# Scores ten groups ahead, the first chunk staged in an idle buffer, and row tiles placed under the weight loads

## The chip, the cores and the metric

The kernel runs on one core of a Trainium2 chip. The metric is the device time of one execution in microseconds. The engines are TensorE (PE, with its weight loads shown apart as PEld), VectorE (DVE), ScalarE (ACT), GpSimd (POOL) and the queue of SyncE (SP), which issues most of the DMAs.

## What is computed

An attention with two mixings over the heads, and two feed-forward parts behind it, all in float32:

```python
# q, k, v: (4, 12, 448, 64); w_pre, w_post: (12, 12)
scores = scale * np.matmul(q, k.transpose(0, 1, 3, 2))
scores = np.einsum('bhij,hg->bgij', scores, w_pre)       # mix of the heads before the softmax
attn   = softmax(scores, axis=-1)
attn   = np.einsum('bhij,hg->bgij', attn, w_post)        # mix of the heads behind it
x      = np.matmul(attn, v)                              # -> (1792, 768)
h      = ((x @ w1) * (x @ w2)) @ w3 @ w_out              # 768 -> 1024 -> 1024 -> 768
out    = leaky_relu(h @ w_in, 0.01) @ w_out2             # 768 -> 2048 -> 768
```

The weights come as float64 and are turned to float32 on the chip.

## The kernel before, in words

**Attention.** Each of the 4 batches is cut into chunks of 120, 120, 120 and 88 query rows, a chunk into blocks of 10 rows, and two blocks make a group: 6, 6, 6 and 5 groups a batch, 92 in all, numbered through. A chunk's scores are made per pair of heads in `qk` (L178): two matmuls into PSUM (L187), eviction into an `s` tile (L183, five buffers; L195 on ACT, L193 on DVE in the start-up), then one DMA per head (`move`, L203 to L215; two for the last head) that lays the 120 rows of that head out so that (row, head) stands on the partitions of a row tile `sr` (L126, three of them in turn). The list `reads` collects these DMAs. `premix` (L236) multiplies a group's row tile by the pre-mixing matrix (L247); it reads a row tile that all 13 moves of the chunk write, so a chunk's first `premix` waits for the last of them. Then `tops` (L257, row maxima on DVE), `softmax` (L264, exponentials on ACT), `weigh` (L269 to L282: sum, reciprocal L274, four scalings L280 and L278, three of them on POOL), `postmix` (L300 on PE, L307 transposes on DVE into an `ap` tile, L291, two buffers) and `av` (L324, the product with v, copied out by L333 and stored to `scr`).

**The loop.** One step takes two groups, k and k+1, for k = 0, 2, ... 90, and a last step k = 92 does only the post-mixing. In the order of PE: `qk` of groups k+LEAD and k+1+LEAD, two to four pairs of `av`, `postmix` of the step before, `premix` of groups k+2 and k+3. The order within attention is written by hand, the same on every engine; an engine and a DMA queue take their instructions in that order. LEAD is 8 (L43); before the loop `qk` runs for the first 8 groups, evicted by ACT and DVE in turn and moved from the queues of ACT and SP. Steps with no `qk` left are called `last` in `weigh`: there one scaling goes to POOL, two to ACT, one to DVE. `marks` (L437) keeps, for each step, its last instruction on each engine.

**Feed-forward.** The first half works on batches 0 and 1, the second on 2 and 3. Each float32 operand is split in a high part (`hi_act`, L72, ACT) and a low part (`lo_dve`, L75, DVE), and a product takes three matmuls. `load_raw` (L81) loads a weight from SP into a `wr` buffer (three), `convert` (L86: L91 on ACT, L92, L93, L96, L99 on DVE) makes a float32 of it, then it is split. `x`, the input of the first half, is loaded from `scr` behind the moves `reads[-5]` and `reads[-3]` (L651); the first weights behind `reads[-1]` (L654, `fill`). The twelve `halves` of `x` (L646) are placed behind the steps that XMARKS names (L453; -5 is step k = 84, -2 is k = 90), the first weight's conversion behind step k = 90 (L660), the second's behind the end of attention (L662). The feed-forward's tiles lie in the same memory as attention's, each waiting for the tiles under it; the three `wr` buffers lie under row tile 0 (the third reaches a little into tile 1), which is the last chunk's, and the loop's last `premix` (step k = 88) reads it.

Of the kernel before, what the change touches and what calls it, by code (L numbers as in the profile page):

```python
# [8 lines left out]
F32 = mybir.dt.float32  # L9
# [3 lines left out]
ALU = mybir.AluOpType  # L13
# [9 lines left out]
def attention_moe_kernel(ctx: ExitStack, tc, qt, kt, vt, w_pre, w_post, w1, w2, w3t, w_out, w_in2, w_out2, out):  # L23
# [7 lines left out]
    nc = tc.nc  # L31
    B, _, NPAIR, S = kt.shape
# [7 lines left out]
    JP = 112  # L40
    NJ = S // JP
    IB = 10
    LEAD, GAP = 8, 13  # L43
    CH = qt.shape[-1]
    scale = 1.0 / float(D) ** 0.5

# [27 lines left out]
    def lo_dve(dst, src, hi):  # L74
        nc.vector.tensor_tensor(out=dst, in0=src, in1=hi.bitcast(F32), op=ALU.subtract)  # L75
# [30 lines left out]
    def attention():  # L106
        with ExitStack() as es:
            ld = es.enter_context(tc.tile_pool(name="a_ld", bufs=2))
            big = es.enter_context(tc.tile_pool(name="a_big", bufs=1))
            const = es.enter_context(tc.tile_pool(name="a_const", bufs=1))  # L110
            late = es.enter_context(tc.tile_pool(name="a_late", bufs=1))
            wk = es.enter_context(tc.tile_pool(name="a_wk", bufs=3))
# [10 lines left out]
            kpost = const.tile([P, 2, 32], F32, name="kpost")  # L123
            mask = const.tile([P, 2, HQ], F32, name="mask")
            eye = const.tile([P, HQ * GAP], F32, name="eye")
            rows_of = [const.tile([P, CH // IB, S], F32, name=f"sr{i}") for i in range(3)]  # L126
            wrep = const.tile([P, 2, H], F32, name="wrep")

            ones = const.tile([P, P], F32, name="ones")
            nc.vector.memset(ones, 1.0)  # L130

            def constants_load():
                for i, t in enumerate(rows_of):
                    (nc.gpsimd if i else nc.vector).memset(t, 0.0)
                for t in (kpre, kpost, eye):
                    nc.gpsimd.memset(t, 0.0)
                for n, w in enumerate((w_pre, w_post)):
                    nc.sync.dma_start(out=wrep[:, n, :], in_=w)
# [39 lines left out]
            def qk(b, c, p, early=False):  # L178

                m = cols[c]  # L180
                if p == 0:
                    srt[b, c] = rows_of[len(srt) % len(rows_of)]
                t = big.tile([CH, 2, S], F32, tag="s", name="s", bufs=5)  # L183
                pq = [bank([CH, S], "pq") for _ in range(2)]
                for e in range(2):
                    rows = slice(e * D, (e + 1) * D)
                    nc.tensor.matmul(  # L187
                        pq[e][:m], qls[b, c][rows, p, :m], kls[b, p // 2][rows, p % 2, :], start=True, stop=True
                    )
                def out():  # L190
                    for e in range(2):
                        if e and early:
                            nc.vector.tensor_copy(t[:m, e, :], pq[e][:m])  # L193
                        else:
                            nc.scalar.activation(out=t[:m, e, :], in_=pq[e][:m], func=ACTF.Copy)  # L195
                    for e in range(2):
                        move(srt[b, c], t[:m, e, :], 2 * p + e, nc.sync if e or not early else nc.scalar)

                evs.append(out)
                if early:  # L200
                    evict()
# [12 lines left out]
                    )  # L214
                    reads.append(ends["sync"])  # L215

            evs = []

            def evict():
                while evs:  # L220
# [48 lines left out]
            def weigh(ns, sm, e, last):  # L269

                m = len(ns)
                nc.vector.tensor_scalar(out=sm[:, :m], in0=sm[:, :m], scalar1=1e-9, scalar2=None, op0=ALU.add)
                rc = wk.tile([P, 2 * HB], F32, tag="rc", name="rc", bufs=2)
                ends["dve"] = nc.vector.reciprocal(out=rc[:, :m], in_=sm[:, :m])  # L274
                shares = (nc.gpsimd, nc.scalar, nc.vector, nc.scalar) if last else (nc.gpsimd,) * 3 + (nc.vector,)
                for i, eng in enumerate(shares[:m]):
                    if eng is nc.scalar:
                        ends["act"] = eng.activation(out=e[:, i], in_=e[:, i], func=ACTF.Copy, scale=rc[:, i:i + 1])  # L278
                        continue
                    ends["dve" if eng is nc.vector else "pool"] = eng.tensor_scalar(  # L280
                        out=e[:, i], in0=e[:, i], scalar1=rc[:, i:i + 1], scalar2=None, op0=ALU.mult
                    )  # L282
# [163 lines left out]
    def moe():  # L446
# [3 lines left out]
        NH = DM // 2  # L450
        FQ = 4
        KH = KM // 2
        XREADS, XMARKS = (-5, -3), (-5, -5, -4, -4, -4, -4, -3, -3, -3, -2, -2, -2)  # L453
        PARTS = ((0, 512), (512, T - 512))
        TERMS = ((0, 0), (0, 1), (1, 0))

# [3 lines left out]
        def behind(mark):  # L460
            es = ExitStack()
            for e in mark.values():
                es.enter_context(tc.issue_after(e.ins))
            return es
# [56 lines left out]
        def first_half():  # L521
            with ExitStack() as er:
# [123 lines left out]
                def halves(n, kk):  # L646
                    hi, lo = (x[:, kk, i, n * S:(n + 1) * S] for i in range(2))
                    hi_act(hi, lo.bitcast(F32))
                    lo_dve(lo, lo.bitcast(F32), hi)

                for n, r in ((0, XREADS[0]), (1, XREADS[1])):  # L651
                    with tc.issue_after(reads[r].ins):
# [3 lines left out]
                for n in range(2):  # L656
                    for kk in range(KM):
                        with behind(marks[XMARKS[n * KM + kk]]):
                            halves(n, kk)
                with behind(marks[-2]):  # L660
                    prepare(1)
                with behind(ends):  # L662
                    prepare(2)
                xx = [x[:, kk] for kk in range(KM)]
                ha, hb = (p.tile([P, KF // 2, 2, T], F32R, tag="h", name="h") for p in (h0, g1))
# [323 lines left out]
```

## Time and profile before

| | us |
|---|---|
| median of 3 runs | 1291.65 (1290.38 to 1298.11) |
| the profiled execution | 1296.13 |
| its span in the trace | 1294.3 |

The profile shows one execution. A row of the timeline gives start, duration, engine, line, operation, output and inputs and the count that was merged, and in brackets how long the engine had been idle and what ended that. "PEclk" is the granted share of TensorE's clock: 1.0 is 2.4 GHz, 0.5 is 1.2 GHz. Attention takes about the first 420 us; the first matmuls of the feed-forward start at 427.

### The profile page before, as it was taken

Reading aid. Unit: us, or ns where it says so; the run is one execution under the profiler, and the core shown is the slowest. Engines: PE = TensorE matmul, PEld = TensorE weight load, DVE = VectorE, ACT = ScalarE, POOL = GpSimd, SP = SyncE. Lnnn points to the kernel's source line nnn. Section 1 sums busy time; section 2 is a strip of 40 time slices with the busy share of each in tenths; the row PEclk is TensorE's granted clock in tenths of the full one; section 3 lists DMA queues with packets and bytes.
Section 4 is the critical chain, followed back from the end, with each engine's and each line's share of the span. In section 5 each row is a group of like instructions: output and inputs, shape, how many; then the busy total and the mean of one; then the engine's idle time right before and its main releaser. Section 6 shows DMA issues by size and latency. Waiting matters only on the chain.

```text
span 1294.3 us, 21888 instructions
## 1 busy us (share of the span) xinstructions
PE 1238.5 (96%) x8616; PEld 981.2 (76%) x8616; DVE 889.0 (69%) x1551; ACT 524.0 (40%) x1024; POOL 198.5 (15%) x141
## 2 busy tenths in 40 slices
PE   6989989999887799999999999999999999999998
PEld 3334435444334689999899999999999999999998
DVE  4766667775657899872689587758776748385662
ACT  2655546555444445532245434235233323432220
POOL 3644545654431000000000000000000000000000
PEclk8999889998898899999999999999999999999999
DMA  5745446655342777555976553506423212112012
GB/s 184 202 147 165 141 146 189 199 156 166 118 151 66 236 237 234 181 187 192 341 253 212 176 203 107 182 25 225 134 86 104 86 34 92 55 50 67 25 50 86
DMA packets 123046, 190.48 MB, mean 147 GB/s; under 512 B 19680, under 2 KB 102720, under 8 KB 122560
## 3 DMA queue, kind: packets, MB, share of 16 engines
q1 hardware_dynamic: 121904, 187.37, 44.9%
q10 hardware_dynamic: 1040, 1.72, 0.4%
q8 instruction: 68, 1.11, 0.4%
q14 instruction: 34, 0.28, 0.1%
HBM read 111.03 MB, written 39.32 MB: 116 GB/s over the span
## 4 chain that ended last, share of the span: by engine, by line
PE 82%; DMA 6%; DVE 6%; ACT 4%; issue 1%; SPq 0%; ACTq 0%; DVEq 0%
PE pm L476 27%; PE po L491 18%; PE pp L766 16%; PE pw L557 5%; DMA sr<-s 5%; PE pq L187 4%; PE pm L247 4%; PE px L324 4%; DVE ap L307 3%; ACT e L264 3%; PE po L300 3%; ACT s L195 1%; DVE mx L257 1%; DMA wr<-in_moe_w_dram 1%; PE turn L234 1%
## 5 line engine op out<-in xcount | busy, mean ns | idle before, releaser
L476 PE MATMUL pm<-x,ws 128*128 128x512 f32 (+1 forms) x1152 | 236.5, 366 | 6.6 <-ACT ws L72 6.4
L476 PEld LDWEIGHTS pm<-x,ws 128*128 128x128 f32 x1152 | 210.6, 189 | 31.7 <-ACT ws L72 6.6
L280 POOL TENSOR_SCALAR e<-e,rc 128x448 f32<-128x448 f32 x130 | 188.5, 1462 | 211.1 <-DVE rc L274 203.2
L264 ACT ACTIVATE e<-pm,mx 128x448 f32<-128x448 f32 x180 | 112.1, 633 | 170.5 <-DVE mx L257 167.1
L247 PE MATMUL pm<-sr,kpre 64*64 64x448 f32 x720 | 100.4, 594 | 32.2 <-DMA sr<-s 20.7
L766 PE MATMUL pp<-t,w 128*128 128x448 f32 x576 | 124.5, 368 | 0.0
L257 DVE TENSOR_REDUCE mx<-pm 128x1 f32<-128x448 f32 x180 | 99.8, 604 | 35.7 <-PE pm L247 35.7
L307 DVE STREAM_TRANSPOSE ap<-po 128x512 f32<-128x512 f32 (+3 forms) x216 | 115.2, 592 | 10.7 <-PE po L300 9.4
L491 PE MATMUL po<-ws,g 128*128 128x384 f32 x672 | 117.2, 334 | 0.0
L491 PE MATMUL po<-wo,g 128*128 128x384 f32 x672 | 117.1, 334 | 0.0
L491 PEld LDWEIGHTS po<-wo,g 128*128 128x128 f32 x672 | 116.6, 188 | 0.2
L491 PEld LDWEIGHTS po<-ws,g 128*128 128x128 f32 x672 | 116.6, 188 | 0.0
L766 PEld LDWEIGHTS pp<-t,w 128*128 128x128 f32 x576 | 108.1, 188 | 10.9
L324 PEld LDWEIGHTS px<-ap,vs 96*64 96x64 f32 (+1 forms) x1536 | 80.9, 141 | 39.1 <-ACT e L264 23.1
L247 PEld LDWEIGHTS pm<-sr,kpre 64*64 64x64 f32 x720 | 27.8, 140 | 103.5 <-issue 49.8
L300 PE MATMUL po<-e,kpost 64*32 64x512 f32 (+1 forms) x1472 | 91.6, 591 | 6.3 <-ACT e L264 5.8
L187 PE MATMUL pq<-kl,ql 64*120 64x448 f32 (+1 forms) x384 | 96.9, 619 | 0.0
L91 ACT ACTIVATE wc<-wr 128x768 f32<-128x768 f32 (+1 forms) x72 | 61.6, 858 | 85.2 <-DMA wr<-in_moe_w_dram 32.4
L324 PE MATMUL px<-ap,vs 96*64 96x120 f32 (+3 forms) x1536 | 90.8, 272 | 5.4 <-DVE ap L307 4.2
L766 PE MATMUL pp<-b,w 128*128 128x448 f32 x432 | 95.6, 368 | 0.0
L195 ACT ACTIVATE s<-pq 120x448 f32<-120x448 f32 (+1 forms) x184 | 86.2, 560 | 20.3 <-PE pq L187 13.2
L498 DVE TENSOR_TENSOR acc<-po,acc 128x384 f32<-128x384 f32 x84 | 45.3, 552 | 66.7 <-PE po L491 66.6
(102 smaller groups left out, 1524.1 us busy)
## 6 DMA issues: line engine op xcount, KB each, us to landing
sr<-s SPq DMA_DIRECT2D x124, 210.0 KB
wr<-in_moe_w_out_dram SPq DMA_DIRECT2D x24, 768.0 KB
wr<-in_moe_w_dram SPq DMA_DIRECT2D x16, 768.0 KB
wr<-in_moe_w_in_dram SPq DMA_DIRECT2D x16, 768.0 KB
wr<-in_moe_w_dram SPq DMA_DIRECT2D x16, 512.0 KB
sr<-s SPq DMA_DIRECT2D x44, 157.5 KB
kept_w<-wc SPq DMA_DIRECT2D x16, 384.0 KB
sa<-kept_w SPq DMA_DIRECT2D x16, 384.0 KB
```

What stands on the lines that cost most here:

```text
L187: nc.tensor.matmul(pq[e][:m], qls[b, c][rows, p, :m], kls[b, p // 2][rows, p % 2, :], start=True, stop=True)
L195: nc.scalar.activation(out=t[:m, e, :], in_=pq[e][:m], func=ACTF.Copy)
L247: nc.tensor.matmul(pms[ns[s % len(ns)]][half:half + Q], kpre[rows], sr[rows, 2 * t + g, :], start=True, stop=True,)
L257: nc.vector.tensor_reduce(out=mxs[n], in_=pms[n], axis=AX.X, op=ALU.max, negate=True)
L264: ends["act"] = nc.scalar.activation(out=e[:, i], in_=pms.pop(n), func=ACTF.Exp, bias=mxs.pop(n), scale=1.0, accum_out=sm[:, i:i + 1])
L280: ends["dve" if eng is nc.vector else "pool"] = eng.tensor_scalar(out=e[:, i], in0=e[:, i], scalar1=rc[:, i:i + 1], scalar2=None, op0=ALU.mult
L300: nc.tensor.matmul(po[g][32 * r:32 * (r + 1), :m], kpost[rows, x], e[rows, :m, JS[r]:JS[r] + P], start=True, stop=True,)
L307: ends["dve"] = nc.vector.transpose(out=dst, in_=po[g][:, i0:i1])
L324: nc.tensor.matmul(px[e * D:(e + 1) * D, r, :nw].rearrange("p (n i) -> p n i", i=HQ), vst[b][rows, jc, 2 * p + e, :], ap[rows, x, :ns, jc, ...
L476: nc.tensor.matmul(dst, wt[:, a, kk, :], x[kk][:, c, c0:c0 + w], start=(kk == order[0] and j == 0), stop=(kk == order[-1] and j == 2),)
L491: nc.tensor.matmul(po, g[m][:, a, t * P:(t + 1) * P], wts[m][:, c, cs], start=(m == 0 and j == 0), stop=(m == FQ - 1 and j == 2),)
L766: nc.tensor.matmul(dst, w[:, i, a, kk, :], b[:, kk, c, :], start=(kk == 0 and j == 0), stop=(kk == KH - 1 and j == 2),)
```

## The change

- LEAD is 10: `qk` runs for ten groups before the loop and for groups k+10 and k+11 in step k. The loads of q and k follow, since their steps are counted from LEAD. The last step with `qk` is k = 80, so five steps are `last`, k = 82 to 90.
- The first chunk's `s` tiles are six slices of one buffer that has the shape and tag of `ap`; the `s` buffers serve from the second chunk on.
- The three row tiles have a pool of their own ahead of the constants, in the order 1, 2, 0. The `wr` buffers now lie under row tile 1 (chunk 13 of 0 to 15, last read in step k = 78) and for a part of the third buffer under row tile 2 (chunk 14, last read in step k = 84).
- In `last` steps the scaling that POOL did is ACT's: three on ACT, one on DVE.
- The low parts of `x`'s halves are made by POOL, and XMARKS spreads them 3, 3, 3, 3 over steps k = 84, 86, 88, 90.
- The first weight is converted behind step k = 88, the second behind step k = 90.

```diff
--- before.py
+++ after.py
@@ -40,7 +40,7 @@
     JP = 112
     NJ = S // JP
     IB = 10
-    LEAD, GAP = 8, 13
+    LEAD, GAP = 10, 13
     CH = qt.shape[-1]
     scale = 1.0 / float(D) ** 0.5
 
@@ -107,6 +107,7 @@
         with ExitStack() as es:
             ld = es.enter_context(tc.tile_pool(name="a_ld", bufs=2))
             big = es.enter_context(tc.tile_pool(name="a_big", bufs=1))
+            rowp = es.enter_context(tc.tile_pool(name="a_rows", bufs=1))
             const = es.enter_context(tc.tile_pool(name="a_const", bufs=1))
             late = es.enter_context(tc.tile_pool(name="a_late", bufs=1))
             wk = es.enter_context(tc.tile_pool(name="a_wk", bufs=3))
@@ -123,14 +124,14 @@
             kpost = const.tile([P, 2, 32], F32, name="kpost")
             mask = const.tile([P, 2, HQ], F32, name="mask")
             eye = const.tile([P, HQ * GAP], F32, name="eye")
-            rows_of = [const.tile([P, CH // IB, S], F32, name=f"sr{i}") for i in range(3)]
+            rows_of = {i: rowp.tile([P, CH // IB, S], F32, name=f"sr{i}") for i in (1, 2, 0)}
             wrep = const.tile([P, 2, H], F32, name="wrep")
 
             ones = const.tile([P, P], F32, name="ones")
             nc.vector.memset(ones, 1.0)
 
             def constants_load():
-                for i, t in enumerate(rows_of):
+                for i, t in sorted(rows_of.items()):
                     (nc.gpsimd if i else nc.vector).memset(t, 0.0)
                 for t in (kpre, kpost, eye):
                     nc.gpsimd.memset(t, 0.0)
@@ -180,7 +181,12 @@
                 m = cols[c]
                 if p == 0:
                     srt[b, c] = rows_of[len(srt) % len(rows_of)]
-                t = big.tile([CH, 2, S], F32, tag="s", name="s", bufs=5)
+                if (b, c) == order[0]:
+                    if p == 0:
+                        staged.append(late.tile([CH, H, S], F32, tag="ap", name="s", bufs=2))
+                    t = staged[0][:, 2 * p:2 * p + 2]
+                else:
+                    t = big.tile([CH, 2, S], F32, tag="s", name="s", bufs=5)
                 pq = [bank([CH, S], "pq") for _ in range(2)]
                 for e in range(2):
                     rows = slice(e * D, (e + 1) * D)
@@ -214,7 +220,7 @@
                     )
                     reads.append(ends["sync"])
 
-            evs = []
+            evs, staged = [], []
 
             def evict():
                 while evs:
@@ -272,7 +278,7 @@
                 nc.vector.tensor_scalar(out=sm[:, :m], in0=sm[:, :m], scalar1=1e-9, scalar2=None, op0=ALU.add)
                 rc = wk.tile([P, 2 * HB], F32, tag="rc", name="rc", bufs=2)
                 ends["dve"] = nc.vector.reciprocal(out=rc[:, :m], in_=sm[:, :m])
-                shares = (nc.gpsimd, nc.scalar, nc.vector, nc.scalar) if last else (nc.gpsimd,) * 3 + (nc.vector,)
+                shares = (nc.scalar, nc.scalar, nc.vector, nc.scalar) if last else (nc.gpsimd,) * 3 + (nc.vector,)
                 for i, eng in enumerate(shares[:m]):
                     if eng is nc.scalar:
                         ends["act"] = eng.activation(out=e[:, i], in_=e[:, i], func=ACTF.Copy, scale=rc[:, i:i + 1])
@@ -450,7 +456,7 @@
         NH = DM // 2
         FQ = 4
         KH = KM // 2
-        XREADS, XMARKS = (-5, -3), (-5, -5, -4, -4, -4, -4, -3, -3, -3, -2, -2, -2)
+        XREADS, XMARKS = (-5, -3), (-5, -5, -5, -4, -4, -4, -3, -3, -3, -2, -2, -2)
         PARTS = ((0, 512), (512, T - 512))
         TERMS = ((0, 0), (0, 1), (1, 0))
 
@@ -646,7 +652,7 @@
                 def halves(n, kk):
                     hi, lo = (x[:, kk, i, n * S:(n + 1) * S] for i in range(2))
                     hi_act(hi, lo.bitcast(F32))
-                    lo_dve(lo, lo.bitcast(F32), hi)
+                    nc.gpsimd.tensor_tensor(out=lo, in0=lo.bitcast(F32), in1=hi.bitcast(F32), op=ALU.subtract)
 
                 for n, r in ((0, XREADS[0]), (1, XREADS[1])):
                     with tc.issue_after(reads[r].ins):
@@ -657,9 +663,9 @@
                     for kk in range(KM):
                         with behind(marks[XMARKS[n * KM + kk]]):
                             halves(n, kk)
+                with behind(marks[-3]):
+                    prepare(1)
                 with behind(marks[-2]):
-                    prepare(1)
-                with behind(ends):
                     prepare(2)
                 xx = [x[:, kk] for kk in range(KM)]
                 ha, hb = (p.tile([P, KF // 2, 2, T], F32R, tag="h", name="h") for p in (h0, g1))
```

## Rows read from the trace of the kernel before

**Rows 1.** The page: granted clock in 40 slices of 32 us

```profile
PEclk8999889998898899999999999999999999999999
```

**Rows 2.** Windows: stretch, length, busy us (instructions) per engine, PEclk, DMA share, GB/s

```profile
108.15:212.03 103.88, 94.48 (x1050) 41.90 (x1050) 68.03 (x157) 52.45 (x143) 52.00 (x36) 0.92 0.51 152
205.28:293.20 87.92, 87.79 (x1092) 41.73 (x1090) 67.65 (x147) 51.90 (x145) 52.00 (x36) 1.00 0.61 184
293.20:369.79 76.59, 68.06 (x684) 28.88 (x684) 45.16 (x102) 35.15 (x95) 34.61 (x24) 0.87 0.42 124
...
408.15:429.00 20.85, 11.24 (x175) 9.15 (x170) 14.74 (x29) 5.81 (x9) 1.59 (x1) 0.77 0.56 175
429.00:433.00 4.00, 3.99 (x9) 3.15 (x10) 3.96 (x6) 2.53 (x3) 0.00 (x0) 0.50 0.95 296
```

**Rows 3.** Timeline of PE: `premix` behind a wait, in batches 0 and 1

```profile
70.71 4.07 PE L247 MATMUL pm<-sr,kpre 64*64 64x448 f32 x16 [3.28 <-DMA sr<-s]
...
168.14 1.99 PE L247 MATMUL pm<-sr,kpre 64*64 64x448 f32 x8 [3.38 <-DMA sr<-s]
```

**Rows 4.** Timeline of SP and PE around one such wait

```profile
135.06 4.20 SPq L212 DMA_DIRECT2D sr<-s  x5
...
140.07 3.15 PE L247 MATMUL pm<-sr,kpre 64*64 64x448 f32 x8 [2.74 <-ACT e L264]
```

**Rows 5.** Timeline and waits of the start-up

```profile
8.38 15.72 SPq L212 DMA_DIRECT2D sr<-s  x9
...
26.04 3.25 PE L247 MATMUL pm<-sr,kpre 64*64 64x448 f32 x12 [0.70 <-DMA sr<-s]
...
DVE s L193 <- DMA sr<-s: 2.9, 1, 2.9
```

**Rows 6.** Windows of the start-up and behind the wait at 70.71

```profile
18.00:26.00 8.00, 1.76 (x4) 0.32 (x4) 1.25 (x2) 1.09 (x2) 0.00 (x0) 0.62 0.62 191
...
71.00:76.00 5.00, 5.00 (x24) 1.60 (x20) 2.40 (x4) 2.59 (x7) 0.00 (x0) 0.66 0.51 152
```

**Rows 7.** Timeline of the last steps: reciprocals (L274), `x` halves

```profile
369.86 0.18 DVE L274 RECIPROCAL rc<-sm 128x4 f32<-128x4 f32 x1
...
385.81 1.04 ACT L72 ACTIVATE x<-x 128x448 fp32r<-128x448 f32 x2 [5.70 <-issue]
...
391.08 0.18 DVE L274 RECIPROCAL rc<-sm 128x4 f32<-128x4 f32 x1
...
394.40 2.19 DVE L75 TENSOR_TENSOR x<-x 128x448 fp32r<-128x448 f32 x4
...
400.10 0.18 DVE L274 RECIPROCAL rc<-sm 128x4 f32<-128x4 f32 x1
...
408.22 0.17 DVE L274 RECIPROCAL rc<-sm 128x3 f32<-128x3 f32 x1
```

**Rows 8.** Groups of DVE, 369.79 to 429: count | busy us, mean ns | idle before

```profile
L96 DVE SCALAR_TENSOR_TENSOR wc<-wr,wc 128x768 uint32<-128x768 uint32 x2 | 1.9, 954 | 0.0
L92 DVE TENSOR_SCALAR wc<-wc 128x768 f32<-128x768 f32 x3 | 1.7, 560 | 5.0 <-ACT wc L91 5.0
...
L75 DVE TENSOR_TENSOR ws<-wc,ws 128x768 fp32r<-128x768 f32 x1 | 0.9, 950 | 0.0
...
L272 DVE TENSOR_SCALAR sm<-sm 128x4 f32<-128x4 f32 (+1 forms) x4 | 0.7, 170 | 4.4 <-ACT e L264 4.4
```

**Rows 9.** Groups of POOL, 110 to 360

```profile
L280 POOL TENSOR_SCALAR e<-e,rc 128x448 f32<-128x448 f32 x91 | 131.5, 1458 | 123.6 <-DVE rc L274 117.8 <-ACT s L195 5.8
```

**Rows 10.** Timeline from the last step to the feed-forward

```profile
401.11 13.30 SPq L228 DMA_DIRECT2D scr<-y  x2
...
414.45 1.53 SPq L83 DMA_DIRECT2D wr<-in_moe_w_dram  x2
...
414.83 5.67 PE L324 MATMUL px<-ap,vs 96*64 96x90 f32 x96 [2.97 <-DVE ap L307]
...
429.01 21.22 PE L476 MATMUL pm<-x,ws 128*128 128x512 f32 x93 [0.20 <-DVE ws L75]
```

## The prediction, made before the changed kernel ran

> **What bounds the kernel now.** I read the page first. TensorE is busy nearly throughout, but its granted clock is not: the row of 40 slices shows full speed from slice 14 to the last, and dips only ahead of that, in attention [rows 1]. From 433 us on the feed-forward is one chain of matmuls at full clock to the end of the span at 1294.3 (861.3 us), and nothing in the change shortens a matmul. So the question is when that chain can start. The second view are windows by stretch of attention [rows 2]. The three stretches begin and end at a step's reciprocal; POOL does three scalings a step there, so its counts of 36, 36 and 24 say 12, 12 and 8 steps. Batch 2 takes 87.92 us for 12 steps, 7.33 each, with PE busy 87.79 of them at clock 1.00: PE sets the pace. Batch 1 takes 103.88 for as many, at clock 0.92, and 9.4 us of it PE is idle; the eight steps of batch 3 take 76.59 at 0.87, 8.5 idle. The work is the same, so batches 1 and 3 lose something that batch 2 does not.
>
> The third view, the timeline of PE, says what. PE waits up to 3.4 us in front of a `premix` six times in these two batches, and once in batch 0; the rows show the one of batch 0 and the longest of the six [rows 3]. SP and PE together give the reason [rows 4]: the moves of step k = 26 are issued from 135.06 to 139.26, and the `premix` behind them goes on at 140.07. The profile names ACT there, which had long been done; the last thing late is the last move. The code says why it is these six. A chunk whose first group f is odd has its first `premix` in step f-3, and with LEAD 8 the `qk` of its last group, f+5, stands in that same step. For f even the step of `qk` is f-4 and that of `premix` f-2, one step between. Chunks of six groups with f odd are 23, 29, 35 and 69, 75, 81: six chunks, six waits. Batches 0 and 2 have even f. After each wait the clock is granted at 0.5 for a while (1.2 GHz), so the price is more than the wait.
>
> **LEAD 10.** Every `qk` stands one step (7.33 us) earlier against its `premix`. Odd chunks come to the one step between that even ones have now, and batch 2, at a DMA share of 0.61, shows no such wait with it [rows 2]. I let batches 1 and 3 run at batch 2's pace: 103.88 - 87.92 = 16.0, and 76.59 - 8 x 7.33 = 18.0, together **33.9 us**. A check from below: idle PE, 9.4 + 8.5, and half-clock time, 0.08 x 103.88 + 0.13 x 76.59 = 18.3, make 36.2.
>
> In batch 0 the chunk at f = 12 is even and still waits 3.28 us [rows 3], with loads of k, q and v in the queues; then 5.0 us run at 0.66, which costs 0.34 x 5.0 = 1.7 [rows 6]. Moves a step earlier cover it: **5.0 us**. Behind that the q and k loads move a step earlier too and keep their distance to use.
>
> Ahead of the loop two more pairs are scored. PE waits for the first chunk's moves until 26.04 [rows 5], and the DMA share stands at 0.62 for all that time [rows 6]. In the start-up 17 moves take the queues from 8.3 to 26.0, about 1.1 us a head; four more heads are 4.4 us if they stand ahead of the first `premix`, and nothing behind it. They are issued behind the first chunk's on both queues, so I take nothing, bounds 0 and +4.4.
>
> The Trainium skill says in "DMA: Bandwidth & Descriptors", section "Why a DMA increments its semaphore by 16 and not by 1", that a DMA runs on the largest number of engines up to 16 which divides both sides' slowest dimension. A move's is 10, so ten of sixteen would be a full house at 0.625, and the row's 0.62 agrees: the idle share is no room for the added moves, and by that rule they cost 4.4 us wherever they get ahead, never less.
>
> **The staged first chunk.** With five `s` buffers the start-up shows one wait for a buffer, 2.9 us on DVE [rows 5], and it is the last pair's, which belongs to the second chunk. With ten groups and no staging, more pairs would wait. Its gain here is 0, at most those 2.9; taken as 0.
>
> **The last steps.** From 369.86 to 408.22 four step intervals take 38.36 us [rows 7]. With LEAD 10 none of them has `qk`. Two things stretch them now. ACT stands 5.70 us in front of the first halves of `x`, since the load of `x` is issued behind the last moves and the halves behind the next step; LEAD 10 brings that load a whole step ahead of the halves. And DVE makes the low parts between the transposes and the row maxima, 2.19 us in the interval from 391.08 to 400.10, which is 9.02 long. Without them that is 6.83, and I take it for each interval: 4 x 6.83 = 27.3, less 0.6 for the three maxima in the last instead of four. The scaling that goes to ACT and the spread of the halves fit into ACT's wait for the maxima. The first weight's conversion comes in now: on DVE twice 0.56, twice 0.95 and the low part 0.95, 4.0 us [rows 8] (the other lines of the conversion are of the same forms). DVE idles 1.1 us a step in front of the sum (4.4 over four steps), so 2.9 show. 27.3 - 0.6 + 2.9 = 29.6, a gain of **8.7 us**.
>
> **From the last reciprocal to the feed-forward.** Now 20.8 us, 408.22 to 429.01, though attention's last matmuls end at 414.83 + 5.67 = 420.50 [rows 10]. The weights' loads are late twice over: under row tile 0 they wait for the last `premix`, and in SP's queue two stores of y stand ahead until 414.41. After, `wr` lies under tile 1, free some 30 us earlier, and the load is right behind that of `x`. PE then goes on when its own `av` is done: 12.3 us behind the reciprocal, as now. The second weight's conversion (4.0) may stand in front of the last transposes, the low parts (1.7) go from there: 10.6 to 14.6, taken 12.3, gain **8.5 us**. The 4.0 us at 0.5 from 429 to 433 [rows 2], which follow PE's idle time, fall away: **2.0 us**.
>
> **POOL's low parts.** The trace has no subtraction on POOL. Nearest is its scaling of the same 128 x 448 with one tensor in, 1.46 us [rows 9]; two tensors in may take that again, 2.9. Twelve of them from step k = 84 on have about 33 us until PE wants all of `x`: 2.8 us each is hidden, so I take 0, with 12 x 0.1 at the upper bound.
>
> Sum: 33.9 + 5.0 + 8.7 + 8.5 + 2.0 = 58.1. Against the profiled execution's 1296.1 (4.5 above the median shown) that is **1238 us**.
>
> **Rivals.** *The weights gain nothing.* Conversions placed by the scheduler among attention's last instructions hold up the transposes, or the loads still stand behind the stores of y, so that the change does not do what it says here. For it: DVE is busy most of the last steps already. Against: the loads' buffers are free early. The 8.5 and 2.0 go: 1248.5.
>
> *POOL and DVE hold each other up.* A DVE scaling in each of four steps and five conversion instructions could each wait for a POOL subtraction of 1.5 us: 13 us at most, say 10, so 1248. No row here has both at once on SBUF. The Trainium skill, "SBUF — State Buffer", section "SBUF: two separate sides", has the pair of ports shared by DVE and POOL as an exclusive lock for a whole instruction; that is this rival, and nothing in the trace decides it.
>
> *Moves stay late.* Four heads a step take about 4.4 us of the move queues, and loads stand among them; a step's lead is then not always enough, as at 70.71 [rows 3]. Half of 33.9 + 5.0 stays: 1257.5.
>
> *POOL decides, to the slower side.* If a subtraction takes p us, the feed-forward starts 12 p - 33 later than forecast. It takes back all 58 from p = 7.6 on, five times the scaling [rows 9]; at p = 9 the time is 1313.
>
> **How the numbers follow.** Chances: the forecast 0.60 (1228 to 1244); the weights gain nothing or the port 0.22 (to 1252); moves stay late 0.12 (to 1262); still less comes of it, within 1%, 0.03; POOL slow 0.03. The low end is 1238 less 2.9 (staging), 2.9 (the conversion wholly hidden), 1.7 (the shorter tail) and the 4.5 by which this execution stands above the median: 1226. The high end takes in late moves and the start-up's 4.4 more: 1262. Measurement tells about 1% from no change; beyond 1% faster is below 1279: 0.94, within 1% 0.03, slower 0.03.
>
> **What would show it.** Right: no wait of PE in front of `premix` behind 30 us; clock 1.00 from there to the last steps; steps of batch 1 at 7.3 us; the ACT wait at the first halves gone; POOL subtractions under 2.8 us; feed-forward matmuls straight behind the last `av`, near 373 us. Wrong: a wait for moves that returns a step later, conversions ahead of the last transposes, a start of the loop later than 27 us, or a feed-forward no longer one chain.

## The result, and the profile after

The changed kernel takes **1235.53 us** (1233.22 to 1235.97), the kernel before, run beside it on the same chip, 1292.78 (1290.38 to 1298.11). The ratio is 0.9548, with a 95% interval from 0.9515 to 0.9581. The forecast was 1238. The profiled execution took 1235.79, with a span of 1234.0, so 60.3 us less than the profiled one of before; the sum had 58.1.

The page first, its span and the granted clock in 40 slices. The dips ahead of slice 14 in [rows 1] are gone; what is left is the start and one slice around 360 us.

```profile
span 1234.0 us, 21876 instructions
...
PEclk8999999999989999999999999999999999999999
```

Next the windows of the kernel after, cut at the reciprocals of the same steps as in [rows 2, 7] (stretch, length, busy us and count per engine, granted clock, DMA share, GB/s): batch 0, the twelve steps k = 22 to 44, the eleven to k = 66, the eight to k = 82, the last four intervals, the tail up to the feed-forward's chain of matmuls, the feed-forward.

```profile
30.20:100.70 70.50, 69.16 (x766) 29.84 (x763) 53.43 (x112) 44.36 (x123) 43.53 (x30) 0.98 0.67 192
100.70:187.07 86.37, 85.64 (x1050) 39.85 (x1050) 67.50 (x157) 51.27 (x143) 52.08 (x36) 1.00 0.61 184
187.07:267.29 80.22, 80.11 (x1015) 38.31 (x1011) 62.16 (x132) 48.20 (x135) 47.72 (x33) 1.00 0.63 187
267.29:324.69 57.40, 57.09 (x734) 26.26 (x736) 44.43 (x102) 34.41 (x96) 34.66 (x24) 1.00 0.55 167
324.69:351.80 27.11, 25.35 (x326) 12.28 (x327) 22.54 (x55) 21.04 (x51) 10.07 (x9) 1.00 0.49 159
351.80:370.08 18.28, 10.31 (x186) 9.00 (x182) 16.69 (x29) 8.12 (x12) 3.67 (x3) 0.81 0.66 218
370.08:1234.00 863.92, 860.01 (x4466) 805.15 (x4464) 601.05 (x931) 307.29 (x453) 0.00 (x0) 1.00 0.42 141
```

Against the same stretches of before, and against the sum of the prediction:

| stretch | before | after | gain | foretold |
|---|---|---|---|---|
| start to the first reciprocal | 30.96 | 30.20 | 0.8 | 0 |
| batch 0 (30.96 to 108.15 before) | 77.19 | 70.50 | 6.7 | 5.0 |
| 12 steps, batch 1 | 103.88 | 86.37 | 17.5 | 16.0 |
| 11 steps, batch 2 (212.03 to 293.20 before) | 81.17 | 80.22 | 0.9 | 0 |
| 8 steps, batch 3 | 76.59 | 57.40 | 19.2 | 18.0 |
| last four intervals | 38.36 | 27.11 | 11.3 | 8.7 |
| last reciprocal to the feed-forward | 20.85 | 18.28 | 2.6 | 8.5 |
| feed-forward to the end of the span | 865.3 | 863.9 | 1.4 | 2.0 |

So the total came out right with one term far off: the tail gave 2.6 and not 8.5, and the terms ahead of it gave 8.7 more than foretold.

**The premix waits are gone.** This is the whole list of PE's waits between 30 and 324 us in the kernel after (who waits, for what, us in total, times, longest). Before, `premix` waited for moves at f = 12 and at the six odd chunks ([rows 3, 4] show three of these seven) and, shortly, at f = 6 (1.41 us at 46.36 and 0.59 at 47.92); now no entry names a DMA.

```profile
PE po L306 <- POOL e L286: 1.0, 2, 0.6
PE px L330 <- ACT e L270: 0.9, 3, 0.3
PE pm L253 <- issue: 0.5, 1, 0.5
```

**The last steps.** Timeline of ACT and POOL in step k = 84 and the group of POOL's subtractions after 320 us (count, then busy us and mean ns). The first halves of `x` follow the three scalings without the 5.70 us of [rows 7], and one subtraction on POOL takes 1.17 us, below its own one-input scaling of 1.46 in [rows 9].

```profile
333.86 1.50 ACT L72 ACTIVATE x<-x 128x448 fp32r<-128x448 f32 x3
...
334.50 3.34 POOL L655 TENSOR_TENSOR x<-x 128x448 fp32r<-128x448 f32 x3 [13.85 <-DMA x<-scr]
...
L655 POOL TENSOR_TENSOR x<-x 128x448 fp32r<-128x448 f32 x12 | 13.7, 1170 | 23.1 <-DMA x<-scr 13.9 <-ACT x L72 9.3
```

**The tail.** Timelines of SP, PE and DVE of the kernel after, from the last moves to the feed-forward. They answer to [rows 10]; the line set apart at the end is of the kernel before.

```profile
326.45 20.53 SPq L234 DMA_DIRECT2D scr<-y  x2
347.03 1.52 SPq L83 DMA_DIRECT2D wr<-in_moe_w_dram  x2
...
354.82 1.52 PE L306 MATMUL po<-e,kpost 64*32 64x384 f32 x32
364.31 5.84 PE L330 MATMUL px<-ap,vs 96*64 96x90 f32 x96 [7.97 <-DVE ap L313]
370.08 2.10 PE L482 MATMUL pm<-x,ws 128*128 128x512 f32 x8
...
352.70 1.30 DVE L313 STREAM_TRANSPOSE ap<-po 128x512 f32<-128x512 f32 x2
355.56 0.97 DVE L92 TENSOR_SCALAR wc<-wc 128x768 f32<-128x768 f32 x1 [1.55 <-ACT wc L91]
356.45 1.30 DVE L313 STREAM_TRANSPOSE ap<-po 128x512 f32<-128x512 f32 x2
...
361.57 0.94 DVE L96 SCALAR_TENSOR_TENSOR wc<-wr,wc 128x768 uint32<-128x768 uint32 x1
362.44 0.40 DVE L339 COPY y<-px 128x240 f32<-128x240 f32 x1
362.76 0.54 DVE L93 TENSOR_SCALAR wc<-wc 128x768 uint32<-128x768 uint32 x1
363.22 1.03 DVE L313 STREAM_TRANSPOSE ap<-po 128x384 f32<-128x384 f32 x2
```

```profile
426.94 1.86 PE L476 MATMUL pm<-x,ws 128*128 128x512 f32 x4 [6.44 <-ACT ws L72]
```

The weight loads are issued at 347.03, not right behind the loads of `x` at 325: two stores of `y` stand ahead in SP's queue and hold it for 20.53 us. DVE's order then has conversions between the last transposes. It waits 1.55 us for the first of them, makes one transpose pair, then conversions and copies from 357.68 to 363.22, and only there the next pair. PE waits 7.97 us for it. Before, PE waited 2.97 us in front of this `av` and 6.44 behind it for the first weight; after, it waits 7.97 in front and not behind. So the conversions no longer follow `av` but hold up its transposes, and the clock is at 0.81 in that window.

The theories after this reading, by the letters that the expectations use. A: LEAD carries nearly all of the gain, by the step that it puts between the last `qk` and the first `premix`. Of the price of a wait, D says that a good part is the half clock behind it, E that it is the wait alone. Of the tail, F says that conversions on DVE in front of the last transposes hold it, G that what counts there is how soon the weights load and convert. H says that low parts on DVE would show in the last steps, I that the tail hides them. J is that staging is hidden.

### The profile page after: what moved, and what is told of

Its sections match the earlier page's. It is cut to its first block, busy times and chain, and to the rows that moved or that the text cites. A ratio compares the mean times of both kernels' runs of the same rounds, so it can differ in the third digit from the quotient of the medians.

```text
span 1234.0 us, 21876 instructions
## 1 busy us (share of the span) xinstructions
PE 1210.2 (98%) x8616; PEld 973.2 (79%) x8616; DVE 882.1 (71%) x1541; ACT 524.2 (42%) x1029; POOL 201.7 (16%) x146
## 4 chain that ended last, share of the span: by engine, by line
PE 88%; DVE 5%; ACT 3%; DMA 2%; issue 1%; ACTq 0%; SPq 0%; DVEq 0%
PE pm L482 28%; PE po L497 19%; PE pp L772 17%; PE pw L563 5%; PE px L330 5%; PE pq L193 4%; PE po L306 4%; PE pm L253 4%; DVE ap L313 3%; ACT e L270 2%; DMA sr<-s 1%; DVE mx L263 1%; ACT s L201 1%; DMA vs<-in_v_dram 1%; DMA scr<-y 1%; PE turn L240 1%
## 5 line engine op out<-in xcount | busy, mean ns | idle before, releaser
L482 PE MATMUL pm<-x,ws 128*128 128x384 f32 (+1 forms) x1152 | 233.6, 363 | 0.0
L286 POOL TENSOR_SCALAR e<-e,rc 128x448 f32<-128x448 f32 x123 | 178.0, 1460 | 132.1 <-DVE rc L280 129.6
L253 PE MATMUL pm<-sr,kpre 64*64 64x448 f32 x720 | 87.5, 565 | 6.7 <-DMA sr<-s 5.6
L193 PE MATMUL pq<-kl,ql 64*120 64x448 f32 (+1 forms) x384 | 88.1, 568 | 1.0 <-ACT s L201 1.0
L772 PEld LDWEIGHTS pp<-b,w 128*128 128x128 f32 x432 | 81.0, 188 | 8.0
```

The lines of the kernel that those rows point to most:

```text
L193: nc.tensor.matmul(pq[e][:m], qls[b, c][rows, p, :m], kls[b, p // 2][rows, p % 2, :], start=True, stop=True)
L253: nc.tensor.matmul(pms[ns[s % len(ns)]][half:half + Q], kpre[rows], sr[rows, 2 * t + g, :], start=True, stop=True,)
L482: nc.tensor.matmul(dst, wt[:, a, kk, :], x[kk][:, c, c0:c0 + w], start=(kk == order[0] and j == 0), stop=(kk == order[-1] and j == 2),)
L772: nc.tensor.matmul(dst, w[:, i, a, kk, :], b[:, kk, c, :], start=(kk == 0 and j == 0), stop=(kk == KH - 1 and j == 2),)
```

## The experiments: LEAD

All comparisons below are with the kernel before, run on the same chip in the same set; its median was 1291.51 for e1 to e4, 1294.93 for e5 to e8 and 1292.92 for e9 to e11.

**e1, before with LEAD 10 and nothing else.**

```diff
 # before
-    LEAD, GAP = 8, 13
+    LEAD, GAP = 10, 13
```

> The kernel before with LEAD 10 and nothing else of the change. Theory A (the moves of a chunk with an odd first group stood in the same step as the premix that reads them; the x load stood one step too late): the six waits and the one of batch 0 go, batches 1 and 3 run at clock 1.00, and the 5.7 us wait at the first halves of x goes; about 45 + 5 us of the change's 57 come from this one number, 1293 - 50 = 1243 us (1239 to 1249). Rival B (the waits are a shortage of DMA time, and the staging or the POOL work is needed to get the gain): half of the waits stay, 1265 or more.

Measured 1243.21 (1242.57 to 1244.3), ratio 0.9623 (0.9607 to 0.964). Its windows of the twelve steps, the eight, and the last four intervals, and PE at the start of the feed-forward:

```profile
100.17:185.72 85.55, 85.29 (x1050) 39.94 (x1050) 67.39 (x157) 51.28 (x143) 52.09 (x36) 1.00 0.62 186
265.93:323.02 57.09, 56.78 (x730) 26.10 (x728) 44.43 (x102) 34.42 (x96) 34.65 (x24) 1.00 0.56 168
323.02:355.25 32.23, 28.25 (x350) 13.41 (x344) 27.33 (x64) 18.79 (x47) 6.37 (x4) 1.00 0.33 110
...
374.03 1.86 PE L476 MATMUL pm<-x,ws 128*128 128x512 f32 x4 [6.41 <-ACT ws L72]
```

One constant gives 48.3 us; all edits together gave 57.3 (1292.78 - 1235.53) beside their own run of before. The two stretches are as short as with all edits (86.37 and 57.40). The last intervals take 32.23 against 27.11: those 5.1 are what the edits to the last steps bring there. The feed-forward waits 6.41 us for its weight: in this kernel the loads stand behind three stores of `y`.

**e2, after with LEAD 9.** The parity rule says that one step between the last `qk` and the first `premix` is enough, and that 9 gives it to odd and even chunks alike.

```diff
 # after
-    LEAD, GAP = 10, 13
+    LEAD, GAP = 9, 13
```

> The changed kernel with LEAD 9. For an odd first group f the last qk moves to step f-5, one step ahead of the premix in f-3; for an even f it stays in f-4, as with LEAD 8. Theory A (it is the parity of f against the steps): the six waits of batches 1 and 3 are gone although the lead grew by one group only; the wait of batch 0 at f = 12 is back (3.3 us and about 1.7 of half clock), and the x load is late again, since step k = 82 has scores again (about 5 us): 1245 us (1240 to 1250). Rival B (each group of lead buys a part of the waits): about half of them stay, 1258 us or more.

Measured 1238.52 (1237.47 to 1240.76), ratio 0.9588 (0.9569 to 0.9608). Windows of the twelve and the eight steps, then PE at the chunk f = 12, and ACT at the first halves of `x`:

```profile
100.04:186.63 86.59, 86.08 (x1048) 39.97 (x1038) 67.36 (x157) 51.27 (x143) 52.08 (x36) 1.00 0.62 184
266.81:322.50 55.69, 55.38 (x709) 26.03 (x710) 44.32 (x102) 33.82 (x95) 34.65 (x24) 1.00 0.58 175
...
64.69 2.37 PE L253 MATMUL pm<-sr,kpre 64*64 64x448 f32 x16 [1.47 <-DMA kl<-in_k_dram]
...
335.91 1.51 ACT L72 ACTIVATE x<-x 128x448 fp32r<-128x448 f32 x3 [3.94 <-issue]
```

The six waits go with the ninth group; the tenth takes the 1.47 us at f = 12 and the wait for `x`. That was foretold in kind and too large: the tenth is worth 3 to 4 us (1238.52 against 1235.53, or gains of 53.0 and 57.3 in their sets), and 1245 had been expected.

**e3, after with LEAD 8**, all other edits kept.

```diff
 # after
-    LEAD, GAP = 10, 13
+    LEAD, GAP = 8, 13
```

> The changed kernel with LEAD 8, all other edits kept. Theory A: the six waits, the wait of batch 0 and the wait for the x load are back, so what is left of the gain is the tail and the low parts of x on POOL: 1235.5 + 45 + 5 = 1286 us (1279 to 1291). Rival C (the other edits carry a good part of the gain): 1270 or less.

Measured 1286.22 (1283.94 to 1288.96), ratio 0.9958 (0.9944 to 0.9972). PE's waits from 30 to 420 us of this kernel, two of the list's lines:

```profile
PE pm L253 <- ACT e L270: 15.8, 6, 3.1
PE px L330 <- DVE ap L313: 9.0, 2, 8.0
```

The six waits are back, as is the 8.0 of the tail. All edits without LEAD give 5.3 us, so 48.3 and 5.3 make 53.6 of the 57.3. The medians of the kernel before differ by 3.4 between the sets, so the 3.7 that are missing don't show that the two parts interact, nor that they don't.

**e4 and e11, before with dummy matmuls in the six waits.** The row tile arrives as late as before, but PE has something to do until then. This tells the half clock apart from the wait.

```diff
 # before; e4 has turn(6), e11 turn(9)
                     if g < NG:
+                        if g in (23, 29, 35, 69, 75, 81):
+                            turn(9)
                         premix(g)
```

> The kernel before with six dummy products (twelve matmul instructions, some 2.6 us at full clock) put on TensorE ahead of each of the six premix that wait for their moves; the results are not used. Theory D (behind each wait the clock is at 0.5 and that costs as much as the wait itself, about 18 us for the six): the wait stays but the clock stays at 1.00, 1293 - 17 = 1276 us (1270 to 1283). Rival E (the half clock behind the wait is hidden by DVE and ACT, only the wait costs): no change, 1290 to 1296.

> As the run with dummy products on the kernel before, nine in place of six ahead of each of the six premix (eighteen instructions, 3.9 us at full clock), longer than the longest of the six waits. Six left 0.5 to 1.4 us of idle and the clock still fell in some places; theory D (idle time is what lets the clock fall, and the half clock behind the waits costs some 18 us): with the wait filled it stays at 1.00 in batches 1 and 3, less up to 1 us each by which the filling is too long: 1277 us (1272 to 1283). Rival E (the half clock costs nothing, and six dummies gained by chance): 1288 or more.

Measured with six 1284.43 (1278.72 to 1284.98), ratio 0.9943 (0.9923 to 0.9963), between the two theories and nearer D; its stretches took 99.88 and 70.16 us, both at a clock of 0.98. With nine 1281.29 (1280.3 to 1284.08), ratio 0.9915 (0.9883 to 0.9947), as D expected. Windows of the twelve and the eight steps of e11, the dummies' group in the first, and one set of them in the timeline:

```profile
104.91:204.66 99.75, 96.62 (x1104) 46.96 (x1104) 68.14 (x157) 52.17 (x143) 52.07 (x36) 0.98 0.54 157
285.52:353.53 68.01, 65.45 (x738) 31.88 (x738) 45.18 (x102) 34.49 (x95) 34.65 (x24) 1.00 0.48 140
...
L234 PE MATMUL turn<-ones 128*128 128x128 f32 x54 | 6.8, 281 | 0.0
...
134.15 2.27 PE L234 MATMUL turn<-ones 128*128 128x128 f32 x18
```

Before, the two stretches made 180.47 us [rows 2]; here 167.76, 12.7 less, though nothing arrives sooner. Idle PE and dummies together are 99.75 - 96.62 + 68.01 - 65.45 + 2 x 6.8 = 19.3 (the second window has the same 6.8) against 17.9 idle before, so the wait itself is nearly unchanged; eighteen dummies took 2.27 us and not the 3.9 expected, so they leave part of each wait idle. PE's own work fell from 162.5 to 96.62 + 65.45 - 13.6 = 148.5, by 14.1. That is half clock given back without touching a single move. The after kernel goes on to 143.77, where the waits go too. So the price had two parts of like size, as the check in the prediction had it. (The trace of e4 is of a run of 1278.72; its other three took 1284.13 to 1284.98.)

## The experiments: the tail and the small edits

**e5, after once more,** beside the next three, with no edit.

> The changed kernel once more, beside the others of this group: 1235.5 us.

Measured 1235.89 (1235.56 to 1237.18), ratio 0.9546 (0.9527 to 0.9566). PE waits 7.96 us in front of the last `av` here too.

**e6, after with the row tiles where they were,** among the constants, in the order 0, 1, 2.

```diff
 # after; the pool a_rows goes too
-            rows_of = {i: rowp.tile([P, CH // IB, S], F32, name=f"sr{i}") for i in (1, 2, 0)}
+            rows_of = {i: const.tile([P, CH // IB, S], F32, name=f"sr{i}") for i in (0, 1, 2)}
```

> The changed kernel with the three row tiles back in the pool of constants, in the order 0, 1, 2, so that the weight buffers lie under row tile 0 again. Theory F (the placement brings nothing, since the loads stand behind a store of y in SP's queue until 347 us and the conversions they allow only get in the way of the last transposes): within 3 us of 1235.5. Rival G (as the change intends, sooner loads mean a sooner start): 1242 us or more.

Measured 1235.65 (1234.44 to 1236.35), ratio 0.9542 (0.9522 to 0.9561): the same time. G is out, but more happens here than that nothing changes. Timelines of SP and PE of this kernel:

```profile
325.11 29.06 SPq L233 DMA_DIRECT2D scr<-y  x3
354.22 1.53 SPq L83 DMA_DIRECT2D wr<-in_moe_w_dram  x2
...
354.71 4.11 PE L329 MATMUL px<-ap,vs 96*64 96x90 f32 x96 [0.55 <-DVE ap L312]
366.85 1.86 PE L481 MATMUL pm<-x,ws 128*128 128x512 f32 x4 [8.03 <-ACT ws L72]
```

The loads now stand behind three stores, 7 us later by the two timelines; in this kernel's order the conversions come behind the last transposes, so `av` runs at once, and PE waits 8.03 us behind it for the weight. Against this kernel, the place of the row tiles moves the same eight microseconds from behind `av` to ahead of it. By this, early loads are of use only if their conversions stay out of the transposes' way; e7 tries that.

**e7, after with the first weight's conversion behind the last step,** the second's behind the low part of the first, and the next ones behind the low part of the second.

```diff
 # after; lo_dve appends its instruction to lows_made
-                with behind(marks[-3]):
+                with behind(marks[-1]):
                     prepare(1)
-                with behind(marks[-2]):
-                    prepare(2)
+                for n in (2, 3):
+                    with tc.issue_after(lows_made[-1].ins):
+                        prepare(n)
```

> The changed kernel with the first weight's conversion put behind the last transposes of attention, and those of the next weights behind it. Theory F (conversions among the last transposes keep TensorE idle for 8 us, 356.3 to 364.3, and at half clock for 6.8): the last av starts at about 357, the feed-forward at about 363 instead of 370, 1235.5 - 7 = 1228.5 us (1226 to 1231). Rival G (a later conversion starts the feed-forward later): 1237 to 1242.

Measured **1227.48** (1225.81 to 1228.51), ratio 0.9478 (0.9457 to 0.9499), faster than both kernels. Timelines of SP, DVE and PE of this kernel; its last reciprocal is at 348.24:

```profile
343.47 1.52 SPq L85 DMA_DIRECT2D wr<-in_moe_w_dram  x2
...
352.23 1.98 DVE L315 STREAM_TRANSPOSE ap<-po 128x384 f32<-128x384 f32 x4
354.13 0.52 DVE L94 TENSOR_SCALAR wc<-wc 128x768 f32<-128x768 f32 x1
...
353.33 4.11 PE L332 MATMUL px<-ap,vs 96*64 96x90 f32 x96 [0.55 <-DVE ap L315]
358.28 4.02 PE L484 MATMUL pm<-x,ws 128*128 128x512 f32 x16 [0.84 <-ACT ws L72]
```

All transposes first, then the conversion, which takes place under `av`: the feed-forward starts 10.0 us behind the last reciprocal, not 18.28, and waits 0.84. The difference is 7.4 us of wait in front of `av` (7.97 - 0.55) and 1.7 of half clock in it (5.84 - 4.11), less the 0.84. This is the tail that the prediction described, but for the first weight's conversion, which it had put ahead of the reciprocal. The loads come as they do in the after kernel, 4.8 us ahead of that reciprocal in both. Against e6, whose loads come late, it is 8.2 us; the two kernels differ in the place of the row tiles and in the conversions' marks, so what the place alone is worth once the conversions wait is not shown. No run has e7's marks with the old place.

**e8, after with the conversions at before's marks,** each one step later.

```diff
 # after
-                with behind(marks[-3]):
+                with behind(marks[-2]):
                     prepare(1)
-                with behind(marks[-2]):
+                with behind(ends):
                     prepare(2)
```

> The changed kernel with the conversions behind the marks of the kernel before (first weight behind step k = 90, second behind attention's end). Theory F: the first weight and a weight with no mark of its own still get in between the last transposes, some 6 us of DVE; the wait is shorter than 8 us by 2 to 5: 1231 to 1235. Rival G (the earlier marks are a part of the gain): 1238 or more.

Measured 1234.96 (1234.01 to 1235.67), ratio 0.9535 (0.9512 to 0.9559). PE still waits, 6.77 us, in front of the last `av`. Moving the marks by one step isn't enough. A mark gives the earliest place of an instruction and does not say what must go first: the second weight's conversion now follows the last transposes, but those of the first weight and of the third, which has no mark, still come between them.

**e9, after with the low parts of `x` on DVE.**

```diff
 # after
-                    nc.gpsimd.tensor_tensor(out=lo, in0=lo.bitcast(F32), in1=hi.bitcast(F32), op=ALU.subtract)
+                    lo_dve(lo, lo.bitcast(F32), hi)
```

> The changed kernel with the low parts of x back on VectorE, three a step. Theory H (in the last steps the transposes, the low parts and the row maxima stand one behind the other on VectorE, and 3 x 0.55 us a step is on the path): the intervals between the reciprocals of steps 84 to 90 grow from 6.8 to 8.4, together 5 us, 1235.6 + 5 = 1240.5 us (1239 to 1244). Rival I (POOL's subtractions of 1.1 us and the shared port cost as much as they save): 1234 to 1237.

Measured 1237.62 (1236.68 to 1239.62), ratio 0.9579 (0.9544 to 0.9614). Its window of the last three intervals, then PE at the last `av`; in the kernel after the same intervals, from 331.83 to 351.80, take 19.97.

```profile
329.99:354.78 24.79, 21.17 (x256) 9.90 (x253) 21.45 (x49) 16.91 (x41) 0.00 (x0) 1.00 0.40 127
...
365.47 5.61 PE L330 MATMUL px<-ap,vs 96*64 96x90 f32 x96 [6.99 <-DVE ap L313]
371.01 5.23 PE L482 MATMUL pm<-x,ws 128*128 128x512 f32 x23
```

The time falls between the two theories. The three intervals grow by the 4.8 us of DVE work, as H has it. But the feed-forward starts 371.01 - 354.78 = 16.2 us behind the last reciprocal, not 18.28, so part of the loss is made up there: the weight loads are issued 6.4 us ahead of the last reciprocal (at 348.40) and not 4.8, and DVE does not wait for the first conversion. POOL is worth some 2 us here, which the intervals (0.9544 to 0.9614 against 0.9527 to 0.9566 in e5) do not set clearly apart from nothing.

**e10, after without the staged first chunk.**

```diff
 # after
-                if (b, c) == order[0]:
-                    if p == 0:
-                        staged.append(late.tile([CH, H, S], F32, tag="ap", name="s", bufs=2))
-                    t = staged[0][:, 2 * p:2 * p + 2]
-                else:
-                    t = big.tile([CH, 2, S], F32, tag="s", name="s", bufs=5)
+                t = big.tile([CH, 2, S], F32, tag="s", name="s", bufs=5)
```

> The changed kernel without the staged first chunk: all ten groups ahead of the loop go through the five s buffers. Theory J (the start-up is set by the moves' time on their queues; pairs 5 to 9 find their buffer free, or free about when the queues would take them anyway): 1235 to 1237.5 us, TensorE's wait for the first chunk ends within 1 us of 23.4. Rival K (the staging is what makes ten groups affordable): 1239 or more.

Measured 1234.34 (1233.42 to 1236.91), ratio 0.9551 (0.9521 to 0.9582), no difference from the kernel after. Two of the waits between 8 and 60 us in this kernel, and the first `premix` here and in the kernel after:

```profile
DVE s L194 <- DMA sr<-s: 5.5, 3, 3.3
ACT s L196 <- DMA sr<-s: 2.2, 1, 2.2
```

```profile
23.00 4.92 PE L248 MATMUL pm<-sr,kpre 64*64 64x448 f32 x16 [6.00 <-DMA sr<-s]
```

```profile
23.41 5.13 PE L253 MATMUL pm<-sr,kpre 64*64 64x448 f32 x16 [5.55 <-DMA sr<-s]
```

The buffer waits are there without staging, 7.7 us in all, and hidden: in both kernels the first `premix` waits for the same moves, at 23.0 and 23.4.

## Why the prediction was right, and where it was not

**LEAD 10 on batches 1 and 3, foretold 33.9, measured 36.7: right.** e2 shows that the mechanism is the step between the last `qk` and the first `premix`: nine groups give it, and the six waits are gone. Batch 2's pace was a good price: 86.37 for twelve steps against 87.92. The check from below, idle 17.9 and half clock 18.3, holds in its parts as well: over the two stretches PE's idle time fell from 17.9 to 1.0 and its busy time from 162.5 to 142.7, by 16.9 and 19.8. (The eight steps hold 734 records against 684, since LEAD moves `qk` and `av` between steps, so this split is rough.) The Trainium skill, "TensorE: Matmul & The Clock Gate", section "HAM oscillation — how this bites in real kernels", prices half clock as its time by 1 - 1.2/2.4. The 18.3 comes to the same sum, and the trace's 19.8 is near it. e11, which fills most of the waits and keeps them, got 14.1 of the 19.8 back.

**Batch 0, foretold 5.0, measured 6.7: right.** The wait at f = 12 is gone, and e2 shows that it is the tenth group that covers the last of it: with nine, 1.47 us of the 3.28 remain. The prediction counted one wait in batch 0 and overlooked the 2.0 us at f = 6, which are gone with nine too; they are of the size of the 1.7 that came on top.

**Start-up and staging, foretold 0: right.** The two added pairs do not get ahead of the first `premix`: it starts at 23.41 and runs through, where before it started at 23.58 and went on at 26.04 [rows 5]. The upper bound of 4.4 us was not needed. The first reciprocal of the loop stands at 30.36, 28.67 and 31.50 in the traces of e5, e7 and e8, whose start-up is the same, so the 0.8 in the table says nothing. e10 shows that staging gains nothing.

**The last steps, foretold 8.7, measured 11.3: right in mechanism, one term too many.** The intervals take 27.11, and the prediction had 26.7 for them ahead of the first weight's conversion (4 x 6.83 - 0.6). The mistake was the added 2.9 for that conversion: the weight is not there yet, and the conversion falls into the tail.

**POOL's low parts, foretold 0 at 1.46 to 2.9 us each: right, and the bound was too high.** The subtraction took 1.17. Twelve come to 13.7 us of POOL, with waits in between. The rival that DVE and POOL hold each other up cost nothing in the last steps, which have the length that was worked out without it; but there the subtractions ran beside DVE's transposes and maxima, whose input is in PSUM. Where one ran beside a conversion, both took longer: L92 at 355.56 took 0.97 us (0.52 in e7, where POOL had ended), and POOL's longest subtraction 1.45 against a median of 1.15. In e8 two steps of a conversion took 0.94 and 1.37. By these rows the hold-up is real, at some 0.4 us of DVE in the kernel after and 1.2 in e8. With the subtractions back on DVE, e9 takes 1237.62 against 1235.53 and 1235.89 of the kernel after, in neighbouring sets.

**The tail, foretold 8.5 + 2.0, measured 2.6 + 1.4: wrong.** The failed step is "the load is right behind that of `x`". By the code the buffers are free early, as the prediction says, but in SP's queue the loads come behind two stores of `y` that wait for their data (20.53 us). The second half of the failed step is "PE then goes on when its own `av` is done", with 4.0 us of conversion at most in front of the transposes. There were three weights: the third carries no mark at all, and DVE made 11.7 us of conversion between 351.80 and 370.08 (2.8 + 2.8 + 2.6 + 1.6 + 1.9 in the groups of that window), 6.5 of them ahead of the transposes at 363.22. Conversions ahead of the last transposes were among the prediction's own signs of being wrong. The 10.6 to 14.6 given as bounds did not hold 18.28. The rival "the weights gain nothing" names just this course, both of its ways at once, and it priced it at 10.5 where 6.5 were lost. That the forecast for the total still held is owed to the other side: the last steps without the 2.9, and LEAD with batch 0 and batch 2 giving 5.4 more. The last reciprocal came 8.8 us earlier than foretold (351.80 against 408.22 - 33.9 - 5.0 - 8.7 = 360.6), which is why "near 373" was met (370.08) though PE waited 7.97 us.

What e7 shows is that this step was a matter of order and no more: with the conversions behind the transposes the tail takes 10.0 us, below the lowest bound given, and the total falls by 8.4 (1235.89 to 1227.48). In its trace 8.2 of that lie between the last reciprocal and the feed-forward. The same trace is 3.6 us ahead at that reciprocal and 1.8 behind in the feed-forward. The edit does not explain the first; the traces of the kernel after, e5, e6, e8 and e10 have that reciprocal between 349.27 and 351.92, so most of it can be the difference between single traces. Of the second, 1.23 us are a wait of PE for a later weight's low part, at 375.35, which the kernel after does not have: the conversions that were put back are a little late there.

**What stays open.** 1.4 us in the feed-forward, 0.9 in batch 2. Of the 19.8 us of PE's busy time that went, e11 gets 14.1 back; the rest was not told apart into clock (0.98 in its first stretch) and other causes.

## What to carry to other kernels

When a wait recurs, look for what its places share in the order of the program: here the parity of a chunk's first group named all six, and one more group of lead took them away (e2); each wait cost about as much again in half clock behind it. When a buffer comes free sooner, ask next who stands ahead of the load in its queue, and where the work on the loaded data then falls on the engine that the critical path needs: early data can put a conversion in front of what must go first. A mark that gives the earliest place of some work does not keep it out of the way of what is urgent; put the low-urgency work behind the last urgent instruction of the same engine.

## What the runs showed of the hardware

- POOL's subtraction of two 128 x 448 float32 tensors took 1170 ns, its scaling of one by a per-partition scalar 1458 [rows 9]; DVE does them in 2.19 / 4 = 0.55 us [rows 7] and 0.45 (L286 in the kernel after). The Trainium skill, "GPSIMD Engine Reference", section "3.1 Elementwise — side-by-side cycle accounting", gives 4497 ns for two inputs of 2048 columns and 1.96 times VectorE's time; by column that is an estimate of 0.98 us for 448. The runs show 1.17, and 2.1 times DVE's.
- The granted clock changes while PE stands still: it is 1.00 from 358 to 361 us and 0.50 from 361.30, both within one wait. This is the window of the kernel after around the wait of 7.97 us, which lasts from 356.34 to 364.31:

```profile
361.30:368.10 6.80, 3.79 (x50) 3.79 (x52) 6.80 (x12) 2.38 (x3) 0.00 (x0) 0.50 0.84 241
```

  At 0.50 for 6.80 us, but PE has work in 3.79 of them only: the part of a half-clock stretch that lies in the wait costs nothing more. In the last four intervals, with waits up to 1.14 us, the clock stays at 1.00.
